# A fused attention and expert kernel: its token table in DRAM in rows of 64 bytes instead of 4, and the first expert's weight loads moved to another queue

## The chip, the core and the metric

The program runs on one core of a Trainium2 chip. It has five engines with queues of their own: PE (matrix multiplications), DVE (vector), ACT (scalar), POOL (general purpose) and SP, which here only issues transfers. Transfers issued by SP, ACT and POOL all run on the core's 16 DMA engines. The metric is the device time of one execution in microseconds (us); lower is better.

## The reference, cut to what matters

Three stages follow one another. Attention with a decay gives 2304 token rows of 512; each row goes to the one expert with the highest logit (8 experts); a second feed-forward layer follows on all rows.

```python
def reference(**kw):
    # attention: 4 batches x 8 heads, 576 tokens, head size 64, causal, with a decay from f
    attn_out = _attn_ref(q, k, v, f)
    x = attn_out.transpose(0, 2, 1, 3).reshape(2304, 512)
    # experts: top 1 of 8
    expert_idx = np.argmax(x @ w_gate, axis=1)
    for e in range(8):
        mask = expert_idx == e
        h = np.maximum(x[mask] @ w1[e], 0.0)            # 512 -> 1024
        out[mask] = gate_w[mask, None] * (h @ w2[e])    # 1024 -> 512
    # second layer: a rational function between two matrix products
    h = out @ w_in                                      # 512 -> 2048
    g = (a0 + a1*h + a2*h**2 + a3*h**3) / (1 + |b0|*|h| + |b1|*h**2 + 1e-6)
    return g @ w_out
```

## The kernel before

**Attention** runs over 16 groups of two heads (`g` = 0 to 15). In a group PE makes scores (`st`), ACT takes their exponential into `pt` (L773), POOL masks the diagonal blocks (L777), PE multiplies by the values (`po`, L800), and PE and DVE find the row maxima of groups that come later (`mx`, L703). SP loads q, k and v of later groups (`rk`, `rq`, `v`, `vt`) and puts the row maxima into place as rows of the operand QA (`QA<-mm`, L752). Between these steps stand the slots of other work, each called once or twice in a group: `do_side` takes the next step of routing, `do_pool` the next transfer of POOL.

**Routing.** When a batch of 576 tokens is through attention, its rows go to `x_d` in DRAM (2052 bytes each), DVE computes for every token its place in its expert's list (`gsi`), and five indirect transfers of POOL write the token numbers (`tok`) to these places in the DRAM tensor `table` (L113, 128 tokens each). `table` is filled with a marker at the start (`fill_table`, L158 and L159). After batch 2, in group 13, `tile_map(0, ...)` computes on DVE which tiles of 128 tokens the first three batches already fill; right behind it `fetch_w(0, nc.scalar)` reads the first expert's number (`te`) and loads its weights, eight pieces of 512 KB into the buffers `raw0` to `raw7` (L484).

**Experts.** 22 to 25 tiles of 128 tokens, sorted by expert. For a tile, POOL reads 128 numbers from `table` (`idx`, L425) and gathers the rows from `x_d` (`xg`, L434). ACT and DVE split each weight piece into a high and a low part (`whi` L1019, `wlo` L1020), PE makes `h` (L1070), transposes (`ht`) and `y` (L1091). When a tile begins a new expert, SP loads the next expert's eight pieces into the same buffers as soon as the split has freed them (L485). At the end of a tile SP stores 128 result rows of 2048 bytes to `y_d` and the 128 token numbers to `id_d`, from the same `idx` tile, which the last stage needs to put its rows back in order:

```python
nc.sync.dma_start(out=y_d[ds(o, P), :], in_=ys_t.pop(p))     # L1044
nc.sync.dma_start(out=id_d[ds(o, P), :], in_=idx_t.pop(p))   # L1045
```

In the second half of this stage POOL loads the last stage's first rows (`yl<-y_d`, `id<-id_d`) and weights (`rw<-wi_d`, `rw<-wo_d`), which ACT and POOL split (`wih`, `woh`, L510).

**The last stage** is the second layer in chunks of 512 rows, its output written by indirect transfers with `id`.

What each engine does in which order is written out by hand in the program text; no planner moves anything. A transfer that SP or ACT issues also waits for an earlier transfer of these two queues, since eight semaphores go round among them.

Of the kernel before, what the change touches and what calls it, by code (L numbers as in the profile page):

```python
# [20 lines left out]
P = 128  # L21
# [20 lines left out]
NSURE = 22  # L42
STRIDE = NT
NSLOT = E * STRIDE + NR * P
NSET = 3
NP = 8

# [24 lines left out]
def fused_kernel(tc, q2, k2, v2, f, w_gate, w1, w2, w_in, w_out, a_in, b_in, out):  # L72
    nc = tc.nc
    with ExitStack() as top, tc.manual_schedule():
# [15 lines left out]

        x_d = dram.tile([NT + 1, XW], F32, name="x_d")
        y_d = dram.tile([NT + P, DM], F32, name="y_d")
        id_d = dram.tile([NT + P, 1], I32, name="id_d")
        table = dram.tile([NSLOT, 1], I32, name="table")
        wi_d = dram.tile([DM, FF], F32, name="wi_d")
        wo_d = dram.tile([FF, DM], F32, name="wo_d")
        ch_d = dram.tile([G, NG, 2, S], F32, name="ch_d")
# [39 lines left out]

        ones = R.tile([P, P], F32, name="ones")
        triu = R.tile([P, P], F32, name="triu")
        tok = R.tile([P, B * NB], I32, name="tok")  # L140
        rev = R.tile([P, NB, E], F32, name="rev")
        est = R.tile([P, NB, E], F32, name="est")
        val = R.tile([P, NB, E], F32, name="val")
# [9 lines left out]
        def iota(t, pattern, base=0, mult=0):  # L153
            nc.gpsimd.iota(t, pattern=pattern, base=base, channel_multiplier=mult,
                           allow_small_or_imprecise_dtypes=True)

        def fill_table(fill, zrow):
            nc.vector.memset(fill, NT)  # L158
            nc.sync.dma_start(out=table.rearrange("(p c) o -> p (c o)", p=P), in_=fill)  # L159
            nc.sync.dma_start(out=x_d[NT:NT + 1, :], in_=zrow)  # L160

        def routing_consts():
            nc.gpsimd.memset(ones, 1.0)
            nc.gpsimd.memset(triu, 1.0)
            nc.gpsimd.affine_select(out=triu, in_=triu, pattern=[[1, 128]], compare_op=ALU.is_gt,
                                    fill=0.0, base=0, channel_multiplier=-1)
            iota(tok, [[S, B], [P, NB]], mult=1)
            iota(rev, [[0, NB], [-1, E]], base=E)
            iota(est, [[0, NB], [STRIDE, E]])
            iota(cmp18, [[0, E], [P, 18]])  # L170
            iota(pid, [[1, NR], [0, E]])
            iota(eid, [[0, NR], [1, E]])
            nc.gpsimd.memset(val, 1.0)
            nc.gpsimd.memset(val[64:128, NB - 1, :], 0.0)
            nc.gpsimd.memset(z8, 0.0)
            nc.gpsimd.memset(acc[0][:, 0, :], 0.0)
            nc.vector.memset(qc, 1.0 + 1e-6)
            nc.sync.dma_start(out=ab, in_=a_in.partition_broadcast(P))
            nc.sync.dma_start(out=bb, in_=b_in.partition_broadcast(P))
# [63 lines left out]
            si_t[b] = si  # L243

        def route_c(b, i):
            ins = scatter_to(table, si_t[b][:BS[i], i:i + 1], tok[:BS[i], b * NB + i:b * NB + i + 1], scat_t)
            scat_t.append(ins.ins)

        def route_steps(b):
# [16 lines left out]
        def tile_map(w, b_next):  # L266
# [4 lines left out]
            def tmp(name, shape):  # L271
                return R.tile(shape, F32, name=f"m{w}_{name}")
# [69 lines left out]
            if w == 0:  # L342
                nc.vector.tensor_tensor(out=ge, in0=nv.to_broadcast(bc), in1=cn.to_broadcast(bc), op=ALU.is_ge)
                nc.vector.tensor_reduce(out=nx, in_=ge, axis=AX.X, op=ALU.add)
                nc.vector.tensor_single_scalar(out=nv, in_=nv, scalar=float(NA), op=ALU.is_lt)
            else:
                nb = tmp("nb", bc)
                nc.vector.tensor_tensor(out=ge, in0=nv.to_broadcast(bc), in1=cn.to_broadcast(bc), op=ALU.is_lt)
                nc.vector.tensor_tensor(out=cn2, in0=cn2, in1=nt2, op=ALU.subtract)
                nc.vector.tensor_tensor(out=nb, in0=nv.to_broadcast(bc), in1=cn.to_broadcast(bc), op=ALU.is_ge)  # L350
                nc.vector.tensor_tensor(out=cn2, in0=cn2, in1=nt2, op=ALU.add)
                nc.vector.tensor_tensor(out=nb, in0=nb, in1=ge, op=ALU.mult)
                nc.vector.scalar_tensor_tensor(out=ge, in0=eid, scalar=float(-E), in1=nb, op0=ALU.add, op1=ALU.mult)
                nc.vector.tensor_reduce(out=nx, in_=ge, axis=AX.X, op=ALU.add)
                nc.vector.tensor_single_scalar(out=nv, in_=nx, scalar=0.0, op=ALU.is_lt)
                nc.vector.tensor_scalar_add(nx, nx, float(E))
# [61 lines left out]
        def at(tiles, p):  # L418
            w, i = (0, p) if p < NA else (1, p - NA)
            return tiles[w][0:1, i:i + 1]  # L420

        def fetch_i(p):
            o = nc.gpsimd.value_load(at(t_off, p), min_val=0, max_val=NSLOT - P)
            idx = W.tile([P, 1], I32, tag="idx", name=f"idx{p}", bufs=8)
            ins = nc.gpsimd.dma_start(out=idx, in_=table[ds(o, P), :])  # L425
            for c in scat_t[:(B - 1) * NB] if p < NA else scat_t:
                tc.add_manual_dep(ins.ins, c.name, SYNC, reason="the table's entries")
            idx_t[p] = idx
# [24 lines left out]

        got_i, got_x = set(), set()

        def fetch_w(p, eng=nc.sync):
            e = eng.value_load(at(t_e, p), min_val=0, max_val=E - 1)
            for i in range(NP):
                fetch_piece(i, e, None, eng)


        def fetch_next(p):
# [9 lines left out]
            for k in range(NP):  # L472
                fetch_piece(k, e, nd)

        def fetch_piece(i, e, nd, eng=nc.sync):
            if True:
                if i < 4:
                    src = w1[ds(e, 1), i * P:(i + 1) * P, :].rearrange("a p f -> (a p) f")
                    dst = raw[i]
                else:  # L480
                    src = w2[ds(e, 1), (i - 4) * 256:(i - 3) * 256, :].rearrange("a (c p) d -> p (a c) d", p=P)
                    dst = raw[i].rearrange("p (c d) -> p c d", c=2)
                if nd is None:
                    return eng.dma_start(out=dst, in_=src)  # L484
                return eng.dma_start(out=dst, in_=src, cond=nd)  # L485

        def ffn_head(ffn, pool_, y_d, id_d, wi_d, wo_d):
# [23 lines left out]
            def load_y(ci, chunk, tbs=None):  # L513
                c0, n = chunk
                if not tbs:
                    ffn["y"], ffn["id", ci] = [], []
                for tb in range(n // P) if tbs is None else [tbs]:
                    r = slice(c0 + tb * P, c0 + (tb + 1) * P)
                    t = F0.tile([P, DM], F32, tag="yl", name=f"yl{ci}_{tb}", bufs=4)
                    eng = nc.gpsimd if ffn["head"] else nc.sync  # L520
                    eng.dma_start(out=t, in_=y_d[r, :])
                    ffn["y"].append(t)
                    t = F0.tile([P, 1], I32, tag="id", name=f"id{ci}_{tb}", bufs=8)
                    eng.dma_start(out=t, in_=id_d[r, :])
                    ffn["id", ci].append(t)

            def y_trans(ci, chunk, k):
# [27 lines left out]
        with ExitStack() as sa:  # L555
# [30 lines left out]
            def load_raw(g):  # L586
                load_k(g)
                load_q(g)
# [292 lines left out]
            LEAD = 3  # L881
            for part in range(3):
                max_pass(2, part)
            fill_table(DW.tile([P, 1024], I32, tag="w64t", name="fill", bufs=1)[:, :NSLOT // P], zer[0:1, 0:XW])
            nc.sync.dma_start(out=zero_d.rearrange("r (p c) -> (r p) c", p=4), in_=wide[0:8, 0:GC // 4])
            prep_hi(2)
            load_v(1)
# [17 lines left out]
                            w64_load(i + 1)  # L905


            first_x = [lambda p=p: (got_i.add(p), fetch_i(p)) for p in range(2)]
            first_x += [lambda p=p: (got_x.add(p), fetch_x(p)) for p in range(2)]
            W64 = [[0, 0, 0, 0, 0, 1, 0], [0, 1, 0, 1, 1, 0, 0], [0, 2, 0, 0, 2, 0, 0], [0, 2, 0, 1, 1, 0, 1], [0, 1, 1, 0, 1, 0, 0], [1, 1, 1, 0, 1, 0, 0], [1, 1, 0, 1, 1, 0, 0], [0, 1, 1, 1, 1, 0, 0], [1, 1, 1, 0, 1, 0, 0], [1, 1, 1, 0, 1, 0, 0], [0, 1, 1, 0, 1, 1, 0], [1, 1, 1, 1, 0, 0, 0], [1, 1, 1, 0, 1, 0, 0], [0, 0, 1, 0, 0, 0, 0], [0, 1, 0, 1, 0, 0, 0], [1, 1, 0, 0, 0, 1, 0]]  # L910
            for g in range(NG):
# [33 lines left out]
                    prep_qlo(g + 2)  # L945
                pv(last, (3, 4,))
                norm(last)
                t_pass(mb, 0)
                do_w64(k64[3])
                if g + 1 < NG:  # L950
                    v_gate(g + 1)
                if n and n % H == 0:
                    b = n // H - 1
                    steps, slots, scatters = route_steps(b)
                    if b < B - 2:
                        steps += [lambda: None] * 2
                        steps += [slots[0], lambda c=scatters, f=slots[1]: (f(), pool_side.extend(c))]
                    else:
                        steps += [slots[0], lambda c=scatters, f=slots[1]: (f(), pool_side.extend(c))]
                        steps.append(lambda: (list(tile_map(0, B - 1)), fetch_w(0, nc.scalar), pool_side.extend(first_x)))  # L960
                    side += steps
                often = 2 if n // H == B - 1 else 1
                for _ in range(often):
# [1 line left out]
                t_pass(mb, 1)  # L965
                if g + 2 < NG:
                    load_v(g + 2)
                if g + 3 < NG:
                    prep_hi(g + 3)
                do_w64(k64[4])  # L970
                for _ in range(often):
                    do_pool()
                if n:
                    pv(n, (0, 1, 2, 3,))
                for _ in range(often):
# [6 lines left out]
                do_w64(k64[6])  # L982
                if g + 4 < NG:
                    load_raw(g + 4)
                for _ in range(often):
                    do_pool()
                if g == 2:
# [2 lines left out]
                do_side()  # L990
            while pool_side:
                do_pool()
            fetch_ahead(0, NA)
            pv(NH - 1, range(NB))
            norm(NH - 1)
# [332 lines left out]
```

## Time and profile before

| | |
|---|---|
| median of 3 runs | 1095.89 us (1089.94 to 1097.42) |
| profiled execution, its own time | 1101.91 us |
| its span, first to last instruction | 1100.3 us |
| mean granted TensorE clock | 0.933 of full speed |
| PE busy | 961.6 us (87%) |
| DVE, ACT, POOL busy | 781.2, 600.2, 379.0 us |

The rows below come from the profiled execution, which is 6 us above the median. Line numbers (L484) are those of the kernel before. An arrow out<-in names what an instruction writes and reads. In brackets behind an instruction stands how long its engine stood idle before it and what ended the wait.

### The profile page before, as it was taken

What the parts mean: (1) busy time and instruction counts of PE and PEld (TensorE: products, weight loads), DVE (VectorE), ACT (ScalarE), POOL (GpSimd) and SP (SyncE); (2) the same over time, 40 slices, a digit from 0 to 9 for tenths busy, and PEclk for the clock granted to TensorE, in tenths of its full rate; (3) what the DMA queues carried; (4) which work ended last, traced back from release to release, by engine and by line L of the source; (5) the groups of instructions that cost most, each with busy time, mean ns of one, the idle gap of its engine ahead of it and who ended that gap; (6) DMA issues with size and microseconds to landing.
All of it is one profiled execution on the core that took longest, in us unless ns stands there. A gap on an engine that the chain in (4) does not pass through costs nothing. (4 is left out here: it accounts for less than half of the span.)

```text
span 1100.3 us, 15948 instructions
## 1 busy us (share of the span) xinstructions
PE 961.6 (87%) x4965; PEld 804.7 (73%) x4965; DVE 781.2 (71%) x1412; ACT 600.2 (55%) x928; POOL 379.0 (34%) x452
## 2 busy tenths in 40 slices
PE   4889998975979787987897977989999999999995
PEld 3878887865957565765775755767888888899994
DVE  6696989886357853645255355999988887888983
ACT  6563654532334442445354454778766666677773
POOL 8573756654313111023410002664312312322222
PEclk9896989887889988898998988999999999999998
DMA  5666586879558588666939452320200100010000
GB/s 181 235 206 233 185 245 211 248 177 133 165 191 126 156 251 212 174 121 196 255 50 185 160 173 60 115 77 10 67 1 10 53 16 9 12 39 1 29 1 29
DMA packets 55822, 137.46 MB, mean 125 GB/s; under 512 B 12831, under 2 KB 13255, under 8 KB 53682
## 3 DMA queue, kind: packets, MB, share of 16 engines
q1 hardware_dynamic: 47456, 114.05, 36.0%
q0 software_dynamic: 6592, 18.13, 7.3%
q10 hardware_dynamic: 1682, 4.20, 2.2%
q8 instruction: 41, 0.67, 0.3%
q14 instruction: 51, 0.42, 0.2%
HBM read 171.04 MB, written 23.86 MB: 177 GB/s over the span
## 5 line engine op out<-in xcount | busy, mean ns | idle before, releaser
L1211 POOL TENSOR_TENSOR glo<-s,ghi 128x512 fp32r<-128x512 f32 (+1 forms) x68 | 82.3, 1211 | 258.0 <-ACT ghi L1209 182.2
L1020 DVE TENSOR_TENSOR wlo<-raw,whi 128x1024 fp32r<-128x1024 f32 x88 | 105.9, 1246 | 50.7 <-ACT whi L1019 50.4
L1172 PE MATMUL fh<-yhi,wih 128*128 128x512 f32 (+1 forms) x320 | 121.1, 378 | 5.4 <-DVE s L1189 5.3
L800 PE MATMUL po<-v,pt 128*128 128x80 f32 (+2 forms) x960 | 115.9, 274 | 5.1 <-DVE lgh L811 4.9
L1174 PE MATMUL fh<-yhi,wil 128*128 128x512 f32 (+1 forms) x320 | 119.5, 373 | 0.0
L800 PEld LDWEIGHTS po<-v,pt 128*128 128x128 f32 (+2 forms) x960 | 109.1, 184 | 14.1 <-issue 6.2
L1173 PE MATMUL fh<-ylo,wih 128*128 128x512 f32 (+1 forms) x320 | 119.1, 372 | 0.0
L1019 ACT CAST whi<-raw 128x1024 fp32r<-128x1024 f32 x88 | 87.5, 1047 | 55.5 <-DMA raw<-in_dram 51.9
L1226 PE MATMUL o<-woh,glo 128*128 128x512 f32 x288 | 113.8, 395 | 1.5 <-POOL glo L1211 1.4
L1224 PE MATMUL o<-woh,ghi 128*128 128x512 f32 x288 | 113.3, 393 | 0.0
L1225 PE MATMUL o<-wol,ghi 128*128 128x512 f32 x288 | 112.8, 392 | 0.0
L773 ACT ACTIVATE pt<-st 128x768 f32<-128x768 f32 (+1 forms) x64 | 53.2, 838 | 99.3 <-PE st L770 80.2
L1070 PE MATMUL h<-whi,xhi 128*128 128x512 f32 x176 | 80.0, 454 | 29.1 <-ACT whi L1019 28.0
L1184 ACT ACTIVATE s<-fh 128x512 f32<-128x512 f32 (+1 forms) x80 | 44.3, 554 | 91.3 <-PE fh L1174 91.3
L703 DVE CUSTOM_DVE_ANT_0 junk<-mx,wide 128x512 f32<-128x512 f32 (+3 forms) x128 | 62.4, 487 | 36.3 <-PE mx L720 25.3
L1186 DVE SCALAR_TENSOR_TENSOR s<-s,bab,s 128x512 f32<-128x512 f32 (+1 forms) x80 | 56.4, 705 | 36.8 <-ACT s L1185 36.2
L1070 PE MATMUL h<-whi,xlo 128*128 128x512 f32 x176 | 74.2, 421 | 4.4 <-DVE xlo L1039 4.4
L768 PE MATMUL st<-QB,KB 128*128 128x192 f32 (+3 forms) x208 | 69.0, 348 | 7.1 <-ACT pt L773 7.1
L777 POOL TENSOR_SCALAR_AFFINE_SELECT pt<-pt 128x128 f32<-128x128 f32 x144 | 45.5, 344 | 84.5 <-ACT pt L773 83.6
L1083 DVE TENSOR_TENSOR hlo<-ht,hhi 128x512 fp32r<-128x512 f32 x44 | 30.3, 689 | 59.3 <-ACTq L1028 42.7
L1172 PEld LDWEIGHTS fh<-yhi,wih 128*128 128x128 f32 x320 | 60.7, 190 | 15.1 <-DVE s L1189 5.7
L1070 PEld LDWEIGHTS h<-whi,xhi 128*128 128x128 f32 x176 | 36.0, 204 | 48.6 <-ACT whi L1019 42.1
(233 smaller groups left out, 2374.6 us busy)
## 6 DMA issues: line engine op xcount, KB each, us to landing
raw<-in_dram SPq DMA_DIRECT2D x192, 512.0 KB
w<-in_dram SPq DMA_DIRECT2D x14, 1024.0 KB
rk<-in_dram SPq DMA_DIRECT2D x16, 576.0 KB
rq<-in_dram SPq DMA_DIRECT2D x16, 576.0 KB
v<-in_dram SPq DMA_DIRECT2D x16, 368.5 KB
y_d<-ys SPq DMA_DIRECT2D x22, 256.0 KB
vt<-in_dram SPq DMA_DIRECT2D x16, 320.0 KB
x_d<-xb SPq DMA_DIRECT2D x4, 1026.0 KB
```

The lines of the kernel that those rows point to most:

```text
L768: nc.tensor.matmul(t[:, c:c + w], lhsT=KB[s][:, k0:k0 + P], rhs=QB[s][:, q0 + done:q0 + done + w], start=True, stop=False)
L800: nc.tensor.matmul(po[:BS[i], i, :w], lhsT=pt[r, c:c + BS[i]], rhs=v[r, (h * NB + j) * VW:(h * NB + j) * VW + w], start=(j == 0), stop=(j ...
L1019: nc.scalar.copy(out=w_hi[i], in_=raw[i])
L1020: nc.vector.tensor_tensor(out=w_lo[i], in0=raw[i], in1=w_hi[i].bitcast(F32), op=ALU.subtract)
L1070: nc.tensor.matmul(t, lhsT=x[:, k * P:(k + 1) * P], rhs=w[k][:, c], start=(i == 0), stop=(i == 11))
L1172: nc.tensor.matmul(t[:, :n], lhsT=whi[:, k, c], rhs=hi[:, k, :n], start=(k == 0), stop=False)
L1173: nc.tensor.matmul(t[:, :n], lhsT=whi[:, k, c], rhs=lo[:, k, :n], start=False, stop=False)
L1174: nc.tensor.matmul(t[:, :n], lhsT=wlo[:, k, c], rhs=hi[:, k, :n], start=False, stop=(k == 3))
L1211: eng.tensor_tensor(out=lo, in0=s3, in1=hi.bitcast(F32), op=ALU.subtract)
L1224: nc.tensor.matmul(t, lhsT=hi[:, s], rhs=whi[:, c], start=(u == 0), stop=False)
L1225: nc.tensor.matmul(t, lhsT=hi[:, s], rhs=wlo[:, c], start=False, stop=False)
L1226: nc.tensor.matmul(t, lhsT=lo[:, s], rhs=whi[:, c], start=False, stop=(u == NU - 1))
```

## The change

`table` and `id_d` get rows of 16 integers (64 bytes) instead of one (4 bytes); all 16 hold the same token number. So the fill, the scatters, the reads into `idx`, the stores to `id_d` and the reads from it change their shape. `tok` is no longer made once for all batches but before each batch's first scatter. One temporary tile of the second `tile_map` shares a buffer (`m_g18`), which makes room in SBUF. The first expert's eight loads go from ACT's queue, where they stood together, to SP's, one at a time at the new slots `do_sp`, three in group 13, four in group 14, one in group 15.

```diff
+IW = 16
-        id_d = dram.tile([NT + P, 1], I32, name="id_d")
-        table = dram.tile([NSLOT, 1], I32, name="table")
+        id_d = dram.tile([NT + P, IW], I32, name="id_d")
+        table = dram.tile([NSLOT, IW], I32, name="table")
...
-        tok = R.tile([P, B * NB], I32, name="tok")
+        tok = R.tile([P, NB, IW], I32, name="tok")
...
-            nc.sync.dma_start(out=table.rearrange("(p c) o -> p (c o)", p=P), in_=fill)
+            rows = table.rearrange("(p c) o -> p (c o)", p=P)
+            for c in range(0, NSLOT // P * IW, 1024):
+                w = min(1024, NSLOT // P * IW - c)
+                nc.sync.dma_start(out=rows[:, c:c + w], in_=fill[:, :w])
...
-            iota(tok, [[S, B], [P, NB]], mult=1)
...
         def route_c(b, i):
-            ins = scatter_to(table, si_t[b][:BS[i], i:i + 1], tok[:BS[i], b * NB + i:b * NB + i + 1], scat_t)
+            if i == 0:
+                iota(tok, [[P, NB], [0, IW]], base=b * S, mult=1)
+            ins = scatter_to(table, si_t[b][:BS[i], i:i + 1], tok[:BS[i], i, :], scat_t)
...
-                nb = tmp("nb", bc)
+                nb = R.tile(bc, F32, tag="m_g18", name="m1_nb")
...
-            idx = W.tile([P, 1], I32, tag="idx", name=f"idx{p}", bufs=8)
+            idx = W.tile([P, IW], I32, tag="idx", name=f"idx{p}", bufs=8)
...
-        def fetch_w(p, eng=nc.sync):
-            e = eng.value_load(at(t_e, p), min_val=0, max_val=E - 1)
-            for i in range(NP):
-                fetch_piece(i, e, None, eng)
+        def fetch_w(p, pieces=range(NP)):
+            if pieces[0] == 0:
+                e_w[p] = nc.sync.value_load(at(t_e, p), min_val=0, max_val=E - 1)
+            for i in pieces:
+                fetch_piece(i, e_w[p], None)
...
-                    eng.dma_start(out=t, in_=id_d[r, :])
+                    eng.dma_start(out=t, in_=id_d[r, 0:1])
...
-            fill_table(DW.tile([P, 1024], I32, tag="w64t", name="fill", bufs=1)[:, :NSLOT // P], zer[0:1, 0:XW])
+            fill_table(DW.tile([P, 1024], I32, tag="w64t", name="fill", bufs=1), zer[0:1, 0:XW])
...
+            def do_sp():
+                if sp_side:
+                    sp_side.pop(0)()
+            first_w = [lambda i=i: fetch_w(0, [i]) for i in range(NP)]
...
-                        steps.append(lambda: (list(tile_map(0, B - 1)), fetch_w(0, nc.scalar), pool_side.extend(first_x)))
+                        steps.append(lambda: (list(tile_map(0, B - 1)), sp_side.extend(first_w), pool_side.extend(first_x)))
```

ACT in group 13, before the change: the eight loads stand between the last copy of one group's preparation (`v`) and the exponentials of group 14.

```order
L624 COPY v_2340<-vg_2499 128x5x2x8
L457 TENSOR_LOAD te_100
L457 ISA x2
L484 ISA
L484 DMA raw_85<-in_dram 128x1024
...
L484 DMA raw_92<-in_dram 128x2x512
L773 ACTIVATE pt_164<-st_0_2620 128x768
L773 ACTIVATE pt_164<-st_1_2633 128x768
```

ACT at the same place, after the change.

```order
L633 COPY v_2343<-vg_2502 128x5x2x8
L782 ACTIVATE pt_164<-st_0_2619 128x768
L782 ACTIVATE pt_164<-st_1_2632 128x768
L782 ACTIVATE pt_165<-st_0_2647 128x896
L782 ACTIVATE pt_165<-st_1_2665 128x768
L756 ACTIVATE mm_2689<-mt_2687 9x128
```

The exponentials now follow the copy with nothing between. SP in groups 13 to 15, before the change (`w` and `wo_d` are loads and stores of the last stage's weights, `tnx` the number of the second expert):

```order
L752 DMA QA_157<-mm_2472 1x9x128 x2
L612 DMA v_2583<-in_dram 128x737
L613 DMA vt_2584<-in_dram 128x640
L752 DMA QA_147<-mm_2690 1x9x128 x2
L658 DMA w_13_2712<-in_dram 128x2048
L664 DMA wo_d<-w64m_2695 128x1024
L463 TENSOR_LOAD tnx_106
```

SP at the same place, after the change.

```order
L622 DMA vt_2570<-in_dram 128x640
L464 TENSOR_LOAD te_100
L493 DMA raw_85<-in_dram 128x1024
...
L493 DMA raw_87<-in_dram 128x1024
L761 DMA QA_147<-mm_2689 1x9x128 x2
L493 DMA raw_88<-in_dram 128x1024
L667 DMA w_13_2712<-in_dram 128x2048
...
L673 DMA wo_d<-w64m_2694 128x1024
L493 DMA raw_92<-in_dram 128x2x512
L472 TENSOR_LOAD tnx_106
```

The last group's QA rows now stand behind the read of `te` and three of the eight loads. SP at the start, where group 2's `KA`, group 1's `v` and group 3's `rk` and `rq` follow the fill, before the change:

```order
L159 DMA table<-fill 128x163
L160 DMA x_d<-zer 1x513
L885 DMA zero_d<-wide 8x288
L602 DMA KA_155<-ch_d 2x2x576
L612 DMA v_304<-in_dram 128x737
```

SP at the start, after the change.

```order
L164 DMA table<-fill 128x1024 x2
L164 DMA table<-fill 128x560
L165 DMA x_d<-zer 1x513
L894 DMA zero_d<-wide 8x288
L611 DMA KA_155<-ch_d 2x2x576
L621 DMA v_306<-in_dram 128x737
```

The fill is three transfers with 16 times the bytes, ahead of the same loads.

## Rows read from the trace of the kernel before

**Rows 1.** Windows, the three stages: busy us of each engine, clock, DMA share, GB/s.
```profile
0.00:306.00 306.00, 248.31 (x1748) 227.71 (x1748) 233.07 (x628) 152.35 (x188) 178.66 (x248) 0.88 0.70 201
306.00:668.00 362.00, 304.99 (x1346) 235.55 (x1347) 190.75 (x269) 153.15 (x210) 62.02 (x76) 0.92 0.67 171
668.00:1100.00 432.00, 408.29 (x1872) 341.44 (x1870) 357.36 (x516) 294.67 (x530) 138.36 (x128) 0.98 0.11 33
```

**Rows 2.** Waits of PE in the expert stage: total us, times, longest.
```profile
PE h L1070 <- ACT whi L1019: 28.0, 16, 7.7
PE ht L1080 <- ACT hs L1074: 14.4, 8, 5.8
```

**Rows 3.** Timeline of all engines, 574 to 589 us: start, us, engine, line.
```profile
574.61 0.36 SPq L1045 DMA_DIRECT2D id_d<-idx  x1
577.00 6.29 SPq L485 DMA_DIRECT2D raw<-in_dram  x8
586.89 1.04 ACT L1019 CAST whi<-raw 128x1024 fp32r<-128x1024 f32 x1 [8.04 <-DMA raw<-in_dram]
587.98 0.80 PE L1070 MATMUL h<-whi,xhi 128*128 128x512 f32 x1 [5.59 <-ACT whi L1019]
```

**Rows 4.** Windows of the same stretch, columns as in rows 1.
```profile
578.00:584.00 6.00, 4.39 (x21) 3.26 (x18) 1.66 (x3) 0.59 (x1) 0.00 (x0) 1.00 1.11 53
586.00:592.00 6.00, 3.83 (x7) 1.67 (x7) 3.86 (x4) 4.18 (x4) 0.00 (x0) 0.50 1.03 404
```

**Rows 5.** Timeline of all engines, 256 to 276 us.
```profile
261.21 12.10 ACTq L484 DMA_DIRECT2D raw<-in_dram  x8
...
262.85 0.96 POOL L113 DMA_INDIRECT table<-tok,gsi  x1 [0.22 <-issue]
264.79 0.80 PE L720 MATMUL mx<-KA,QA 128*128 128x512 f32 x1 [3.99 <-DVE M L703]
273.41 1.51 ACT L773 ACTIVATE pt<-st 128x768 f32<-128x768 f32 x2 [18.05 <-DMA raw<-in_dram]
274.27 0.53 PE L768 MATMUL st<-QB,KB 128*128 128x192 f32 x1 [6.88 <-ACT pt L773]
```

**Rows 6.** Tile raw: ns of one issue, min/median/max; first and last start.
```profile
L484 ACTq DMA_DIRECT2D raw<-in_dram x8: 339/379/622, 261.2 to 272.9; - x8
```

**Rows 7.** Windows before the first scatter: loads behind the fill; x_d's rows of 2052 bytes.
```profile
28.00:30.00 2.00, 2.00 (x19) 1.87 (x17) 1.38 (x6) 1.48 (x2) 0.67 (x3) 1.00 1.04 380
142.00:144.00 2.00, 2.00 (x19) 1.86 (x17) 1.89 (x7) 1.72 (x2) 1.27 (x5) 1.00 0.99 130
```

**Rows 8.** Windows behind ACT's loads: the clock.
```profile
277.00:279.00 2.00, 2.00 (x9) 1.70 (x9) 0.54 (x4) 1.00 (x2) 0.78 (x3) 0.50 0.90 126
281.00:283.00 2.00, 2.00 (x21) 1.84 (x21) 0.52 (x2) 1.28 (x2) 0.00 (x0) 1.00 0.91 278
```

**Rows 9.** Timeline of all engines, 22 to 38 us.
```profile
36.03 1.15 ACT L606 CAST KA<-rk 64x1152 fp32r<-64x1152 f32 x1 [2.13 <-DMA rk<-in_dram]
36.67 0.50 PE L770 MATMUL st<-QA,KA 128*128 128x192 f32 x1 [2.22 <-DMA QA<-mm]
```

**Rows 10.** Timeline of all engines, pieces around 386, 438, 498 and 648 us.
```profile
386.52 0.62 PE L1070 MATMUL h<-whi,xhi 128*128 128x512 f32 x1 [2.78 <-ACT whi L1019]
438.87 0.80 PE L1070 MATMUL h<-whi,xhi 128*128 128x512 f32 x1 [7.72 <-ACT whi L1019]
497.27 0.62 ACT L510 CAST wih<-rw 128x512 fp32r<-128x512 f32 x1 [7.20 <-DMA rw<-wi_d]
498.44 1.11 PE L1080 MATMUL ht<-ident,hs 128*128 128x128 f32 x4 [5.79 <-ACT hs L1074]
648.90 0.80 PE L1070 MATMUL h<-whi,xhi 128*128 128x512 f32 x1 [5.89 <-ACT whi L1019]
```

**Rows 11.** Waits of POOL in the expert stage.
```profile
POOL id L524 <- DMA id_d<-idx: 6.1, 1, 6.1
```

**Rows 12.** Window of 20 us around one of PE's gaps.
```profile
580.00:600.00 20.00, 14.22 (x51) 9.59 (x50) 10.18 (x10) 10.10 (x12) 1.71 (x1) 0.74 0.98 234
```

More of the change, by code (lines that the diff above doesn't have):

```diff
@@ L454, in fused_kernel @@
         got_i, got_x = set(), set()
-        def fetch_w(p, eng=nc.sync):
-            e = eng.value_load(at(t_e, p), min_val=0, max_val=E - 1)
-            for i in range(NP):
-                fetch_piece(i, e, None, eng)
+        def fetch_w(p, pieces=range(NP)):
[3 more added lines that the diff above has]
+                fetch_piece(i, e_w[p], None)
+        e_w = {}
         def fetch_next(p):
@@ L473, in fetch_border, with fetch_piece @@
                 fetch_piece(k, e, nd)
-        def fetch_piece(i, e, nd, eng=nc.sync):
+        def fetch_piece(i, e, nd):
             if True:
@@ L483, in fetch_piece @@
                 if nd is None:
-                    return eng.dma_start(out=dst, in_=src)
-                return eng.dma_start(out=dst, in_=src, cond=nd)
+                    return nc.sync.dma_start(out=dst, in_=src)
+                return nc.sync.dma_start(out=dst, in_=src, cond=nd)
         def ffn_head(ffn, pool_, y_d, id_d, wi_d, wo_d):
@@ L905, in do_w64 @@
                             w64_load(i + 1)
+            sp_side = []
+            def do_sp():
+                if sp_side:
+                    sp_side.pop(0)()
+            first_w = [lambda i=i: fetch_w(0, [i]) for i in range(NP)]
             first_x = [lambda p=p: (got_i.add(p), fetch_i(p)) for p in range(2)]
@@ L947, in fused_kernel @@
                 norm(last)
+                do_sp()
                 t_pass(mb, 0)
@@ L967, in fused_kernel @@
                     load_v(g + 2)
+                do_sp()
                 if g + 3 < NG:
@@ L972, in fused_kernel @@
                     do_pool()
+                do_sp()
                 if n:
@@ L984, in fused_kernel @@
                     load_raw(g + 4)
+                do_sp()
                 for _ in range(often):
@@ L992, in fused_kernel @@
                 do_pool()
+            while sp_side:
+                do_sp()
             fetch_ahead(0, NA)
```

## The prediction

> **What bounds the kernel now.** I began with the busy time and clock of the three stages [rows 1]. In the last one PE is busy 408 of 432 us at a clock of 0.98 and the DMA engines are nearly idle; nothing in the change touches it but the shape of `id`, so it stays. The gaps are in the first two. In the expert stage PE stands still for 57 of 362 us at a clock of 0.92, while the DMA engines count as busy for 67% of the stage and move only 171 GB/s.
>
> Next came the waits of PE there [rows 2]: 28.0 us are waits for a weight piece that ACT has just split, and 14.4 us waits for ACT's `hs`. Where ACT waits itself, it waits for the transfer: in [rows 3] its split stood idle for 8.04 us and PE for 5.59 us until the first piece had landed, 9.9 us after SP began to issue it at 577.0. The windows of that stretch [rows 4] show why. From 578 to 584 us the DMA engines have packets open all the time and move 53 GB/s; from 586 on the same loads run at 404. The loads are not slow, they are held up, for 6 to 8 us. Ahead of the hold-up stands the store of 128 token numbers to `id_d`, one row of 4 bytes per token, issued at 574.61.
>
> The same picture is at the end of attention. Scatters of `table` write 4-byte rows to DRAM too; the fourth of a batch is issued at 262.85 us, and ACT's loads of that moment need 12.1 us for eight issues with a median of 0.38 us [rows 5, 6]. Before the first scatter, plain loads move 380 GB/s [rows 7]. One other write slows the engines: the rows of `x_d`, 2052 bytes each, during which 130 GB/s are moved [rows 7]; the change leaves those alone. So I read: a burst of 4-byte rows written to DRAM, many of them neighbours, blocks all DMA engines for 6 to 8 us, and whoever needs a load just then waits.
>
> **The change, part by part.** *The loads leave ACT.* Between 261.21 and 273.31 us ACT does nothing but issue, so the exponentials of group 14 come at 273.41, and PE loses 6.88 us [rows 5]. The 3.99 us that PE lost before, at 264.79, are DVE's, which was in `tile_map`; they stay. The 6.88 us go whole: the first scores of the group are ready at 261, and once ACT can take them nothing else holds PE. The clock is at its lower level until about 281 [rows 8]. PE works at that level from 264.8 to 267.4 and again from 274.3; without the gap the second part follows the first, so some 2.6 us of work at half speed are saved, 1.3 us. Together **8.2 us less**.
>
> The rows show eight issues with a median of 0.379 us [rows 6], 3.0 us of issuing in the 12.1. The Trainium skill, "DMA: Bandwidth & Descriptors", section "Issuing engines are not separate DMA queues", says that which engine issues a transfer matters only for the time of issuing, which is usually small. By that rule the move alone would be worth at most these 3.0 us; the trace does not agree, because the issues wait for earlier transfers and ACT's own work stands behind them.
>
> *They join SP.* The read of `te` there waits for `tile_map`, as it did on ACT, and by 261 us that is over. Queued behind it are the QA rows of the last group, which now follow three pieces, 1.5 MB, 4 us at 380 to 404 GB/s [rows 4, 7]. These rows are made some 10 us later, so this costs nothing; without that cover it would be up to 4 us for the scores of group 15. The pieces are first used behind attention's scores, more than 15 us after the first issue.
>
> *The fill grows* from 83 KB to 20864 rows of 64 bytes, 1.34 MB. At 380 GB/s [rows 7] that is 3.5 us of all DMA engines against 0.2. It stands ahead of group 1's and 3's loads in SP's queue, and these were late already: ACT waited 2.13 us for `rk`, PE 2.22 us for the QA rows behind it [rows 9]. So there is no cover: **3.3 us more**, from 2 (the engines are not full when it starts) to 5 (two further issues and a longer memset come first).
>
> *Small edits.* `tok` is remade four times on POOL, a fraction of a microsecond each and long after the scatters that read it last; the shared temporary is written and read by DVE alone, in order; `idx` and `id` keep their 128 rows. Zero, or 1 us together if POOL were late.
>
> *The rows of 64 bytes.* No write of 64-byte rows is in this trace. The two ends are that the hold-up stays as it is, or that it goes. The nearest row on the good side is the fill's own, 652 bytes each, with loads at 380 GB/s behind it; on the bad side stand `x_d`'s rows, at 130 GB/s [rows 7]. [...]
>
> What that gives: four of PE's 16 waits for pieces, at 386.52, 438.87, 587.98 and 648.90, make 22.0 of the 28.0 us [rows 2, 3, 10], each no longer than a hold-up. At 587.98 the first piece would land some 3.5 us after its issue (512 KB at 404 GB/s [rows 4] is 1.3 us, and I allow 2 to land) instead of 9.9, which is 6.4 us earlier and more than the wait. Of the other 6.0 us, in twelve waits, I count 2; the rest is the pace of the pieces, 1.3 us each, where an expert has one tile only. That makes 24. Of the waits for `hs`, 5.79 us come from ACT waiting 7.20 us for `rw` [rows 10], which POOL issued late because it had waited 6.1 us for a store to `id_d` [rows 11]; I count 6 of 14.4. That is 30 us. The 20 us around the gap at 588 have a clock of 0.74 [rows 12], so 10 of them at the lower level, half of these with PE at work, which lost 2.5 us; with four such gaps 10 us, of which I count 5. Against that I set 4 us for what is next late (`wlo`, the split itself). **31 us less**, from 12 to 48 as bounds.
>
> Sum: 1101.9 - 8.2 + 3.3 - 31 = 1066.0. The profiled execution's own time lies 6.0 us above the median of the runs, so the forecast is 1060.
>
> **The rivals.** *The rows of 64 bytes hold up the engines as the 4-byte ones do.* Then only ACT's gain and the fill's cost remain: 1101.9 - 8.2 + 3.3 = 1097.0, as a median 1091. For it: no row shows such a write, and `x_d`'s rows slow the engines although they are long. Against: the fill's rows do not. The same page of the Trainium skill, section "Specifications", puts the limit at 512 bytes, below which the DMA engine reads, changes and writes back; by that rule 64 bytes gain nothing and this rival is the result, and none of the rows here shows a write of a size between 4 and 652 bytes to settle it.
>
> *The hold-up goes, but PE gains half of it*, since an expert with one tile still has 4 MB to load, 10.4 us at 404 GB/s, and since ACT's and DVE's splits become late: 15 us less instead of 31, so 1076. For it: from 586 on the loads run at full rate and PE is busy for only 3.83 of 6 us [rows 4].
>
> *Slower: the new rows lengthen the hold-up.* A scatter or a store to `id_d` now touches 128 separate pieces of 64 bytes where it touched some 8 to 16; if each costs what a shared one does, a hold-up of 7 us gets longer. Place: the five gaps of PE in the expert stage [rows 3, 10]. The 4.9 us gained elsewhere are used up when each is 1 us longer, and the time is 1% up from 3.2 us each; doubled, 7 us each, it is 1126. [...]
>
> **How the numbers follow.** Forecast 0.59, half gain 0.14, no gain from the rows 0.19, slower 0.08. The forecast's own spread, from the bounds above, is 1038 to 1082; with the half gain, which lies in it, that holds 0.7. To leave out no more than 2 in 10 the upper end goes to the first rival, 1092. The three runs spread over 0.7%, so about 1% (11 us) is what a measurement can tell from no change. Faster by over 1% are the forecast and the half gain, 0.73; within it lies the first rival, 0.19; slower 0.08.
>
> **What would show it.** In the changed kernel's profile: no issue by ACT between group 13's copy of `v` and the exponentials behind it, and PE's gap of 6.88 us gone; behind each store to `id_d` the loads at 350 GB/s or more instead of some 50; PE's waits for `whi` under 8 us in all; the expert stage's clock above 0.95; the wait for `rk` at the start 3 us longer. Wrong would be GB/s that fall behind the stores to `id_d` as before (first rival), or waits of PE that stay although the loads run at full rate (second).

## The result, and the profile after

The changed kernel takes **1043.8 us** in the median (1039.9 to 1049.0) against 1094.2 us before, a ratio of 0.954 with a 95% interval of 0.949 to 0.960. The forecast was 1060. The profiled execution's own time is 1039.9 us with a span of 1038.3 us, both 62.0 us less than before; 11.6 us of that difference belong to the two executions, since the medians lie 50.4 us apart.

The first view is again the windows of the stages. The rows of after are cut where the first expert's first matmul and the last stage's first matmul start, at 299.0 and 609.0 us; one row of before with the same cut (303.5 and 665.9 us) stands by itself, because [rows 1] were cut at round numbers.

```profile
0.00:299.00 299.00, 247.86 (x1747) 227.37 (x1747) 225.05 (x626) 150.80 (x187) 180.84 (x249) 0.89 0.67 209
299.00:609.00 310.00, 283.77 (x1338) 225.91 (x1338) 190.96 (x270) 154.64 (x212) 66.19 (x79) 0.98 0.60 200
609.00:1038.00 429.00, 408.58 (x1880) 341.70 (x1880) 358.38 (x518) 294.92 (x530) 138.73 (x128) 0.99 0.11 34
```
```profile
303.50:665.90 362.40, 303.36 (x1339) 233.97 (x1339) 192.47 (x270) 154.96 (x212) 64.08 (x78) 0.92 0.67 171
```

Read the expert stage first: 362.4 us became 310.0, which is 52.4 of the 62.0. Subtract PE's busy time from each: PE stood still for 59.0 us before and for 26.2 after. That is 32.8 us of waits. The other 19.6 us are PE's busy time itself, for 1339 matmuls and 1338: the same work at a granted clock of 0.98 in place of 0.92. Attention ends 4.5 us earlier and the last stage is 5 us shorter.

The waits of PE in that stage after the change (total us, times, longest) answer to [rows 2]:

```profile
PE ht L1102 <- ACT hs L1096: 5.4, 6, 2.6
PE h L1092 <- ACT whi L1041: 4.4, 7, 1.3
```

28.0 us became 4.4 and 14.4 became 5.4, together 32.6 of the 32.8. The timeline and a window of the same tile as in [rows 3, 4], now some 44 us earlier, show the cause:

```profile
530.16 0.35 SPq L1067 DMA_DIRECT2D id_d<-idx  x1
...
532.56 5.42 SPq L494 DMA_DIRECT2D raw<-in_dram  x8
...
538.65 1.05 ACT L1041 CAST whi<-raw 128x1024 fp32r<-128x1024 f32 x1 [3.01 <-DMA raw<-in_dram]
...
539.75 0.50 PE L1092 MATMUL h<-whi,xhi 128*128 128x512 f32 x1 [0.60 <-ACT whi L1041]
```
```profile
534.00:540.00 6.00, 5.40 (x26) 4.03 (x25) 2.73 (x5) 2.48 (x5) 0.00 (x0) 1.00 0.91 320
```

The loads behind the store move 320 GB/s where they moved 53, ACT has its first piece 6.1 us after SP began to issue in place of 9.9, and PE's 5.59 us of waiting are 0.60.

The end of attention, against [rows 5]: SP issues the loads in pieces, ACT's exponentials wait for PE's scores alone, and the 6.88 us gap of PE is gone. DVE's 3.99 us stayed, as 4.16.

```profile
267.16 1.43 SPq L493 DMA_DIRECT2D raw<-in_dram  x3
270.83 0.79 PE L729 MATMUL mx<-KA,QA 128*128 128x512 f32 x1 [4.16 <-DVE M L712]
273.10 0.81 ACT L782 ACTIVATE pt<-st 128x768 f32<-128x768 f32 x1 [5.53 <-PE st L779]
```

But DVE's wait itself comes at 270.83 us, 6.0 us later than before. Some of that starts with the fill, against [rows 9]:

```profile
23.82 1.68 SPq L164 DMA_DIRECT2D table<-fill  x3
36.83 1.15 ACT L615 CAST KA<-rk 64x1152 fp32r<-64x1152 f32 x1 [2.85 <-DMA rk<-in_dram]
38.54 0.50 PE L779 MATMUL st<-QA,KA 128*128 128x192 f32 x1 [4.06 <-DMA QA<-mm]
```

and two more waits of PE for the QA rows come in mid-attention, 2.40 us at 160.96 and 2.73 us at 227.04. They follow stores of `x_d` whose code the change leaves alone. The windows of one, issued at 142.6 us, show that it had become slower than in [rows 7], where 130 GB/s were moved:

```profile
146.00:148.00 2.00, 2.00 (x18) 1.86 (x17) 1.87 (x7) 1.71 (x2) 1.29 (x5) 1.00 1.25 76
148.00:150.00 2.00, 2.00 (x20) 1.76 (x20) 1.88 (x3) 2.00 (x4) 1.72 (x1) 1.00 1.02 102
150.00:152.00 2.00, 1.60 (x12) 1.30 (x11) 2.00 (x2) 0.71 (x2) 1.93 (x2) 1.00 1.34 83
152.00:154.00 2.00, 0.92 (x8) 0.95 (x9) 1.93 (x8) 0.00 (x0) 2.00 (x1) 1.00 1.17 60
154.00:156.00 2.00, 2.00 (x15) 2.00 (x15) 1.93 (x4) 0.00 (x0) 0.68 (x3) 0.68 0.73 82
```

For ten us the DMA engines are busy and move 60 to 102 GB/s. So the profile leaves four questions: which of the two parts carries the gain, which of the two arrays, what it is in 4-byte rows that holds up the loads, and why `x_d` became slow.

### The profile page after: what moved, and what is told of

Its sections match the earlier page's. It is cut to its first block, busy times and chain, and to the rows that moved or that the text cites. A ratio compares the mean times of both kernels' runs of the same rounds, so it can differ in the third digit from the quotient of the medians.

```text
span 1038.3 us, 15953 instructions
## 1 busy us (share of the span) xinstructions
PE 940.2 (91%) x4965; PEld 795.0 (77%) x4965; DVE 774.4 (75%) x1412; ACT 600.4 (58%) x928; POOL 385.8 (37%) x455
## 5 line engine op out<-in xcount | busy, mean ns | idle before, releaser
L1092 PE MATMUL h<-whi,xhi 128*128 128x512 f32 x176 | 73.0, 415 | 5.1 <-ACT whi L1041 4.4
L1096 ACT ACTIVATE hs<-h 128x512 f32<-128x512 f32 x44 | 26.3, 597 | 86.2 <-PE h L1092 86.1
L1092 PE MATMUL h<-whi,xlo 128*128 128x512 f32 x176 | 70.4, 400 | 4.4 <-DVE xlo L1061 4.4
L779 PE MATMUL st<-QA,KA 128*128 128x192 f32 (+3 forms) x208 | 63.1, 328 | 9.2 <-DMA QA<-mm 9.2
```

What stands on the lines that cost most here:

```text
L1092: nc.tensor.matmul(t, lhsT=x[:, k * P:(k + 1) * P], rhs=w[k][:, c], start=(i == 0), stop=(i == 11))
```

## Experiments

Every ratio is against runs of the kernel before on the same chip, with its 95% interval.

**Rows alone.** 64-byte rows, with the eight loads back on ACT in one go:

```diff
...
-                        steps.append(lambda: (list(tile_map(0, B - 1)), sp_side.extend(first_w), pool_side.extend(first_x)))
+                        steps.append(lambda: (list(tile_map(0, B - 1)), fetch_w(0, nc.scalar), pool_side.extend(first_x)))
```

> 64-byte rows, with the first expert's eight loads back on ACT in one go. By my reading (the rows carry the gain, the loads about 8 to 10 us of it) this stands 7 to 11 us above the changed kernel, at 1051 to 1055, with ACT's stall of about 12 us in front of the exponentials of group 13 back and the waits on whi still under 8 us in the expert stage. If the loads carry the gain, it stands within 10 us of the kernel before, at 1084 to 1094.

Measured: 1054.8 us, 0.963 (0.958 to 0.968): as expected in size, 40 of the 50 us. The stall is not as expected. In the timeline of this kernel the eight issues take 5.81 us in place of 12.10, and PE loses 0.58 us behind ACT in place of 6.88:

```profile
271.98 5.81 ACTq L492 DMA_DIRECT2D raw<-in_dram  x8
...
278.75 0.53 PE L776 MATMUL st<-QB,KB 128*128 128x192 f32 x1 [0.58 <-ACT pt L781]
```

So most of what I had booked under "the loads leave ACT" was the hold-up too, and here it is that of the scatters, the only rows written beside these loads that got wider: the first store to `id_d` comes after 320 us in both kernels. Windows from one to five us behind the first of these loads, first before the change and then in this kernel, agree:

```profile
262.21:266.21 4.00, 1.43 (x5) 1.33 (x6) 3.46 (x21) 0.00 (x0) 1.38 (x3) 0.71 1.51 37
```
```profile
272.98:276.98 4.00, 1.41 (x5) 1.31 (x6) 3.48 (x21) 0.00 (x0) 1.42 (x3) 0.50 0.84 297
```

Why this kernel is still 11 us behind the changed one is only partly seen. From ACT's copy of `v` ahead of these loads to its next one it takes 22.0 us against 19.8; the expert stage has 2.9 us more idle time of PE and 5.0 us more busy time, at a clock of 0.97; and 4.9 us of the lag are there at 261 us, before any of these loads is issued. The lag in the expert stage has no cause that I can show. The 4.9 us need none in this edit: two kernels further down that differ from the changed one only in `id_d`, which nothing writes before 320 us (4 bytes in rows of 64, and the table alone), reach this copy at 262.6 and 270.4 us, against 261.0 in the changed kernel and 265.9 here.

**Loads alone.** 4-byte rows as before, with `first_w`, `do_sp` and its five calls from the change.

> 4-byte rows as before, with the first expert's loads one by one on SP. By my reading 1083 to 1089, 5 to 11 us below the kernel before: ACT's stall of about 12 us goes, the waits on whi stay near 28 us. If SP's queue now gets the stall and hands it on to the next loads of attention, no gain: 1092 to 1098. If the loads are what the gain is made of: 1045 to 1055.

Measured: 1092.5 us, 0.998 (0.994 to 1.001), a gain of 2.3 us that may be 6.3 or none: short of my 5 to 11, and inside the range that I had named for no gain. The stall of ACT is gone here as well (from ACT's copy of `v` to its next one, 21.2 us against 29.4 before). The waits of PE in the expert stage stay for the most part:

```profile
PE h L1086 <- ACT whi L1035: 21.8, 10, 5.4
PE ht L1096 <- ACT hs L1090: 10.9, 6, 3.7
```

**One array at a time.** First the table alone at 64 bytes, then the token numbers alone, with a table of 4-byte rows and its short fill:

```diff
-        id_d = dram.tile([NT + P, IW], I32, name="id_d")
+        id_d = dram.tile([NT + P, 1], I32, name="id_d")
...
-                nc.sync.dma_start(out=id_d[ds(o, P), :], in_=idx_t.pop(p))
+                nc.sync.dma_start(out=id_d[ds(o, P), :], in_=idx_t.pop(p)[:, 0:1])
```
```diff
+TW = 1
...
-        table = dram.tile([NSLOT, IW], I32, name="table")
+        table = dram.tile([NSLOT, TW], I32, name="table")
...
-            idx = W.tile([P, IW], I32, tag="idx", name=f"idx{p}", bufs=8)
+            idx = W.tile([P, TW], I32, tag="idx", name=f"idx{p}", bufs=8)
...
-                nc.sync.dma_start(out=id_d[ds(o, P), :], in_=idx_t.pop(p))
+                nc.sync.dma_start(out=id_d[ds(o, P), 0:1], in_=idx_t.pop(p))
```

> Rows of 64 bytes in the table alone; the tiles' token numbers go to DRAM in rows of 4 bytes, as before. By my reading the stores of the token numbers, one for each tile, are what holds the loads up in the expert stage: nearly all of the gain there is lost, 1075 to 1090, with waits on whi of 15 us or more. If the table's rows matter more (its scatters and its reads), this stays near the changed kernel, 1044 to 1056.

> Rows of 64 bytes for the tiles' token numbers alone, of which 4 bytes are written; the table has rows of 4 bytes, as before, and so a short fill. By my reading nearly all of the gain is kept, and the fill's cost is saved: 1036 to 1050. If the table matters more: 1070 to 1092.

Measured: the table alone gives 1096.2 us, 0.999 (0.996 to 1.003), nothing, even with the loads on SP, and above the range that I had named. The token numbers alone give 1044.2 us, 0.953 (0.946 to 0.960), everything. The window over the same tile's loads, from one to seven us behind their issue, is first the table's and then the numbers':

```profile
582.00:588.00 6.00, 5.24 (x25) 3.87 (x23) 2.56 (x4) 1.47 (x3) 0.00 (x0) 1.00 0.61 73
```
```profile
536.00:542.00 6.00, 6.00 (x28) 4.44 (x26) 4.06 (x5) 3.77 (x6) 0.00 (x0) 1.00 0.87 295
```

and PE's waits with the table alone are close to those of before:

```profile
PE h L1092 <- ACT whi L1041: 25.0, 11, 7.1
PE ht L1102 <- ACT hs L1096: 14.2, 6, 5.3
```

So the gain comes from the 22 stores of `id_d`. The scatters of 4-byte rows hold loads up as well. From one to five us behind the first load that SP issues at the end of attention, the loads move 35 GB/s with the loads alone (4-byte table) and 318 with the table alone (64-byte):

```profile
263.92:267.92 4.00, 1.34 (x5) 1.25 (x6) 3.48 (x20) 0.00 (x0) 1.85 (x5) 0.78 1.30 35
```
```profile
277.53:281.53 4.00, 1.33 (x5) 1.24 (x5) 3.48 (x20) 0.00 (x0) 1.90 (x5) 0.50 0.96 318
```

But with the loads on SP no engine is seen to wait for these bytes: ACT splits the first piece at 285.9 us in the kernel with the loads alone, 23 us after its issue.

**What in these stores.** Four kernels ask whether it is the size of a write or the distance of the rows, and from which value on. One writes 4 bytes into each row of 64; three change `IW` alone, to 8 (32 bytes), 4 (16 bytes) and 2 (8 bytes).

```diff
-                nc.sync.dma_start(out=id_d[ds(o, P), :], in_=idx_t.pop(p))
+                nc.sync.dma_start(out=id_d[ds(o, P), 0:1], in_=idx_t.pop(p)[:, 0:1])
```

> As the changed kernel, but the store of an expert's token numbers writes only the first 4 bytes of each 64-byte row. If 4-byte writes hold the other transfers up because neighbours share 64 bytes, this is the changed kernel again, within 5 us (1040 to 1049), and behind each such store the loads go at over 350 GB/s. If any write of less than 64 bytes holds them up, the hold-ups of some 6 us behind each of the stores come back: waits on whi of 15 to 28 us in the expert stage, and 1060 to 1085.

> Rows of 32 bytes in both arrays: two neighbours share 64 bytes. If 64 bytes is the step at which the hold-ups end, they come back at least by half: 1060 to 1090. If the cost falls with the number of neighbours in a row of 64 bytes (two in place of sixteen): about an eighth of some 50 us, 1046 to 1054. If 32 bytes is enough, as the changed kernel or up to 2 us below it, for its fill at the start is half as large: 1041 to 1046.

> Rows of 16 bytes in both arrays, four neighbours to 64 bytes. With 32 bytes as fast as 64, two theories are left. A step between 4 and 32 bytes set by the size of one write: at 16 bytes either wholly slow (1075 to 1090) or wholly fast (1032 to 1044). A cost that grows with the number of writes that fall into the same 64 bytes, from two on hardly anything at 32 bytes: in between, 1044 to 1060.

> Rows of 8 bytes in both arrays, eight neighbours to 64 bytes. By the number of neighbours: about half of the gain is gone, 1058 to 1075. By a step at a size above 8 bytes: all but the loads' part is gone, 1083 to 1094.

Measured: 4 bytes in rows of 64 gives 1044.0 us, 0.953 (0.948 to 0.958), the changed kernel again. Rows of 32, 16 and 8 bytes give 1036.5, 1040.1 and 1042.8 us, with ratios of 0.947 (0.940 to 0.953), 0.950 (0.945 to 0.955) and 0.950 (0.946 to 0.955). The 32-byte rows come out below all three ranges that I had given, and all the gain is there at 8 bytes, which neither of my two theories for that kernel expected. The last two kernels of this kind take the 8-byte rows with 4 bytes written, and the 4-byte rows (`IW = 1`) with the 128 numbers of a tile copied as one piece of 512 bytes from the table:

```diff
-                nc.sync.dma_start(out=id_d[ds(o, P), :], in_=idx_t.pop(p))
+                o2 = nc.sync.value_load(at(t_off, p), min_val=0, max_val=NSLOT - P)
+                nc.sync.dma_start(out=id_d[ds(o, P), :].rearrange("p o -> o p"),
+                                  in_=table[ds(o2, P), :].rearrange("p o -> o p"))
```

> Rows of 8 bytes, of which the store of an expert's token numbers writes only the first 4. If the distance of the rows decides, this is the kernel with rows of 8 bytes wholly written: 1039 to 1048. If it is the size of one write that decides once neighbours lie close together, the hold-ups of the 4-byte rows are back: 1075 to 1095, with waits on whi of 15 us or more.

> Rows of 4 bytes in both arrays, loads one by one on SP, but the token numbers of a tile go from the table to their place as one copy inside DRAM, 512 bytes in one row, in place of 128 writes of 4 bytes from SBUF. If the 128 close small writes hold the loads up, the gain is all here without wider rows: 1036 to 1050. If rows of 4 bytes cost in another way (where they lie, how they are read later), it stays at 1080 to 1095.

Measured: 1042.4 us, 0.952 (0.948 to 0.956), and 1050.9 us, 0.961 (0.957 to 0.965), just above its range. The windows over the same tile's loads, in this order: 4 bytes in rows of 64, rows of 32, rows of 16, rows of 8, 4 bytes in rows of 8, one piece of 512.

```profile
540.00:546.00 6.00, 6.00 (x30) 4.71 (x28) 4.35 (x5) 3.84 (x6) 0.00 (x0) 1.00 0.90 305
```
```profile
532.00:538.00 6.00, 6.00 (x29) 4.74 (x28) 4.36 (x6) 3.79 (x6) 0.00 (x0) 1.00 0.91 317
```
```profile
533.00:539.00 6.00, 5.74 (x27) 4.18 (x25) 3.60 (x5) 2.81 (x5) 0.00 (x0) 1.00 0.99 311
```
```profile
534.00:540.00 6.00, 6.00 (x29) 4.52 (x27) 3.83 (x5) 2.96 (x6) 0.00 (x0) 1.00 0.97 314
```
```profile
530.00:536.00 6.00, 6.00 (x29) 4.54 (x27) 4.01 (x5) 3.75 (x6) 0.00 (x0) 1.00 0.90 300
```
```profile
549.00:555.00 6.00, 5.25 (x25) 4.07 (x24) 3.36 (x4) 2.90 (x4) 0.00 (x0) 1.00 0.93 318
```

The last number of each row is 300 to 318 GB/s, against 53 before and 73 with 4-byte token numbers. A write of 4 bytes does no harm 8 or 64 bytes from the next one. The same 512 bytes at the same place do none in one piece. What holds the loads up in the expert stage is a store of 128 writes of 4 bytes that lie directly side by side. The copy in one piece is 7 us slower than the changed kernel all the same. Its profiled execution, at 1058.7 us, lies 7.8 us above its own median, so the trace can't settle why. It shows three things: behind a wait of 2.1 us the 60 matmuls `po` at the end of attention run at a granted clock of 0.50 and take 12.2 us, where the kernel with the loads alone takes 6.7 at 1.00; SP's copy waits for the table's scatters once, for 6.7 us, with SP's other issues queued behind it; and PE's waits for `hs` are 9.1 us in place of 5.4. Which of them it is was not tried.

**The slow stores of `x_d`.** In the changed kernel these stores, of rows of 2052 bytes, had become slow. Two kernels set the rows 2112 bytes apart, so that no two share 64 bytes; the 60 bytes at each row's end are zeroed by one more transfer in attention's third group. One has rows of 64 bytes in table and token numbers, the other rows of 32.

```diff
-XW = DM + 1
+XW = DM + 16
...
+                    nc.sync.dma_start(out=x_d[:NT, DM + 1:].rearrange("(p c) d -> p c d", p=P),
+                                      in_=wide[:, :270].rearrange("p (c d) -> p c d", d=15))
...
```

> The changed kernel, with the rows of x_d 2112 bytes apart in place of 2052, so that no two rows lie in the same 64 bytes; the 60 bytes at each row's end are set to zero by one more transfer in attention's third group. If shared 64 bytes at the rows' ends are why the stores of x_d take some 10 us each, at 40 to 130 GB/s, they now take 3 to 5 us, the waits of TensorE on QA at 160 and 227 us go, and the time is 1034 to 1041. If something else slows these stores, nothing changes but the added transfer: 1043 to 1047.

> Rows of 32 bytes as in the fastest kernel so far (1036.5), with the rows of x_d 2112 bytes apart. Its x_d stores took 4.4 to 6 us already, so by the sharing of 64 bytes at most some 3 us are left to gain: 1033 to 1038. If the added transfer and the longer rows read by the gathers weigh more: 1037 to 1041.

Measured: 1037.8 us, 0.948 (0.945 to 0.951), and 1040.2 us, 0.950 (0.946 to 0.954). In the first, windows over the store that is issued at 143.1 us answer to those shown of the changed kernel:

```profile
146.00:148.00 2.00, 2.00 (x18) 1.86 (x16) 1.75 (x10) 1.61 (x3) 1.14 (x5) 1.00 1.03 307
148.00:150.00 2.00, 2.00 (x22) 1.85 (x20) 1.88 (x4) 2.00 (x4) 1.43 (x2) 1.00 1.02 353
150.00:152.00 2.00, 2.00 (x16) 1.68 (x14) 2.00 (x1) 1.07 (x2) 1.93 (x2) 1.00 1.14 345
```

307 to 353 GB/s in place of 60 to 102. Both mid-attention waits for QA are gone, and the first expert starts at 293.3 us, 5.7 us earlier; the median is 6.0 us lower, while the profiled executions lie only 2.1 us apart, since the expert stage of this one is 3.6 us longer. With rows of 32 bytes nothing is gained on top: the three kernels at 1036.5, 1037.8 and 1040.2 us can't be told apart, and they lie 4 to 7 us below the changed kernel, at the edge of what these runs can tell.

## Why the prediction was right, and where its terms were off

**The hold-up was the cause, and its end the gain.** Of what it said would be seen, all is there but two items. The loads behind a store move 320 GB/s, a little under the 350 named, because the window takes in their start: from 536 to 538 us they move 379, from 538 to 540 us 414. The clock of the expert stage is 0.98, the waits for `whi` are 4.4 us, and ACT's issue is gone from the end of attention. The wait for `rk` at the start is 0.7 us longer, not 3.

**The 31 us for the rows were too small: 52.4 us in the profiled executions.** The waits were well sized: 24 + 6 - 4 = 26 us forecast, 32.8 measured, mostly because the 4 us for "what is next late" did not come. The step that failed is the clock. I took the loss around one gap, 2.5 us, times four, and counted half of that, 5 us in all; PE's busy time fell by 19.6 us. In 20-us windows of before, the clock is below 1.00 in nine of the 18 from 300 to 660 us, and after the change in two of the 16 up to 620 us. I had looked at four large gaps, and a clock of 0.92 over 362 us was in [rows 1] to be multiplied: the time at the lower level is about 0.16 of the stage (half speed there gives 0.92), 58 us, and a good part of it was PE at work. The kernel with the loads alone, whose stage with 4-byte rows took 353.5 us, says the same:

```profile
297.04:650.52 353.48, 301.55 (x1339) 235.20 (x1339) 192.22 (x270) 155.10 (x212) 68.00 (x80) 0.93 0.67 175
```

Against it the changed kernel's stage is 43.5 us shorter, 25.7 of waits, which is what was forecast for them, and 17.8 of PE's busy time. On top came 5 us that I had not seen at all: in the last stage, PE's wait for `s` before the first matmul of the shared part. The row of before, then that of after:

```profile
679.59 0.80 PE L1172 MATMUL fh<-yhi,wih 128*128 128x512 f32 x1 [5.28 <-DVE s L1189]
```
```profile
617.80 0.50 PE L1194 MATMUL fh<-yhi,wih 128*128 128x512 f32 x1 [0.33 <-DVE s L1211]
```

It stays with the loads alone (4.9 us), and is 0.3 us with the table alone widened and 1.7 with the token numbers alone, so it hangs on the rows; what it waited for there was not taken apart.

**"The loads leave ACT", 8.2 us less, was right as a span and wrong as a term.** Between ACT's two copies of `v` the stall's end brings 8.2 us with 4-byte rows. But the median gained only 2.3 us by this part alone, and 11.0 us where the rows were changed already. The two parts don't add: with wide rows most of ACT's stall goes without the move.

**The fill, 3.3 us more.** At the start it is 1.9 us (PE reaches 38.54 us in place of 36.67). That attention is 6.0 us late by 270 us has mostly another cause, on which the prediction said "the change leaves those alone": the stores of `x_d`. With their rows padded, and the long fill kept, ACT's copy of `v` before the first loads comes at 255.3 us, where it came at 255.1 before the change and at 261.0 after it.

**The good end, that the hold-up goes with 64-byte rows, was a choice from rows far away.** The nearest one was the fill's, of 652 bytes, so that it came true has luck in it, and no run shows that 4-byte writes which share 64 bytes have to be merged. In the stores of `id_d` rows of 8 bytes, eight to 64 bytes, do no harm, so sharing 64 bytes is not what decides there. The table's scatters, which the prediction put beside the stores, do hold loads up, as it read; but widening them alone gives no time: no engine is seen to wait for those loads once SP issues them, and the wide table slows the stores of `x_d`.

**The range.** Its lower end, 1038, is not what the bounds of its terms give (1101.9 - 8.2 + 2 - 48 - 6.0 = 1041.7). The result lies inside either.

**The rivals.** No gain from the rows (1091) is excluded by the kernel with wide token numbers alone. The limit of 512 bytes that would make it so (the Trainium skill, "DMA: Bandwidth & Descriptors", section "Specifications") is not the one met here: stores in rows of 8, 16, 32 and 64 bytes leave the loads at 295 to 320 GB/s, and scatters in rows of 32 and 64 bytes leave theirs at 297 to 318. Longer hold-ups (1126) are excluded by the same windows, and "PE gains half" by PE's idle time.

## What to carry to other kernels

Look at what stands ahead of a slow load in DRAM: 512 bytes written as 128 pieces of 4 bytes side by side can hold up 4 MB of loads for 6 us, and twice the row length cured it for this store. Ask also who waits for the loads: the scatters held them up too, and on SP that cost nothing that the medians show. When a gap of PE goes, the granted clock in the stretch behind it can give back more: here 19.6 us on top of 32.8 us of waits. So price it from the stage's mean clock and not gap by gap. Rows whose length is not a multiple of 64 bytes deserve one trial with padding; here the median fell by 6.0 us beside a 64-byte table, at the edge of what the runs can tell, and not at all beside a 32-byte one.

## What the runs showed that I had not expected

That 8 bytes are enough for the time: with rows of 4, 8, 16, 32 and 64 bytes (loads on SP throughout) the medians are 1092.5, 1042.8, 1040.1, 1036.5 and 1043.8 us. Why the step lies between 4 and 8 is open. The scatters have no such step. From one to five us behind the first of the first expert's loads, these move 35 to 39 GB/s with a table of 4-byte rows, 73 to 75 with 8, 174 with 16 and 297 to 318 with 32 or 64; whether the size of a write or the number of neighbours makes this was not tried.

That the width of the table changes how long `x_d`'s stores take, with the same code for them. From 146 to 156 us they run at 60 to 102 GB/s with 64-byte rows; with 32-byte rows the loads behind the store are back at 274 GB/s and more from 146 us on, 7 us after its issue. That it is the table's width, and not that of the token numbers, the kernels with one array each show: from 6 to 12 us behind the issue of this store the DMA engines move 62 to 104 GB/s with the table alone at 64 bytes, and 263 to 394 with the numbers alone. Padding cures it, so the row's length has a part in it. Whether the arrays' places in DRAM, or what else runs beside these stores, makes the difference was not tried.
